# Loading the complex weights of an AFNO layer two modes at a time, in 16 KB runs, with the transform read from two 64-column blocks of x

## The chip, the cores and the metric

The kernel runs on one core of a Trainium2 chip. The metric is the device time of one execution in microseconds (us). The kernel before takes 427.19 us, the median of three runs (427.02 to 427.77). Run to run it moves by about 0.2%.

The engines are PE (TensorE matmul; PEld is its load of the stationary operand), DVE (VectorE), ACT (ScalarE), POOL (GpSimd) and SP (SyncE). The kernel's tiles lie in SBUF, and the results of its matmuls in PSUM, the two memories on the chip; a tile has up to 128 rows, called partitions. The program pins the instructions that matter here (`pin` in the kernel), so that each engine takes them in the order of the program. Nearly all loads are issued by GpSimd and convert f32 to 16 bits on the way; so GpSimd's queue is also the queue of the loads.

## The reference

The layer is linear attention followed by a spectral mix. Batch 8, 8 heads, sequence 576, head size 64, so a model width D of 512. There are 64 Fourier modes, and each has a real and an imaginary weight matrix of 512x512 in f32: together 134 MB, which is most of what is read.

```python
# attention, per batch and head: phi(t) = elu(t) + 1
kv  = einsum('bhsd,bhse->bhde', phi(k), v)
x   = einsum('bhsd,bhde->bhse', phi(q), kv) / (einsum('bhsd,bhd->bhs', phi(q), sum_s phi(k)) + 1e-6)
x   = x.transpose(0, 2, 1, 3).reshape(B, S, 512)
# spectral mix
X   = rfft(x, axis=1)[:, :64]                       # Xr + i Xi
Yr  = einsum('bmd,mde->bme', Xr, w_r) - einsum('bmd,mde->bme', Xi, w_i)
Yi  = einsum('bmd,mde->bme', Xr, w_i) + einsum('bmd,mde->bme', Xi, w_r)
u   = x + irfft(Yr + i Yi, n=576, axis=1)
out = u + relu(u @ w_ch)                            # (8, 576, 512) f32
```

## The kernel before

The program has three parts. Stage A forms x for each of the eight batches and transforms it to the frequency domain (the result is `xt_c`). The stream then multiplies each mode by its weights as they arrive, and fills the gaps with other work. The tail, after the last weight, does the last inverse transforms and the stores.

One load brings one matrix of one mode. Partition p takes rows 4p to 4p+3, that is 4 x 512 f32 = 8 KB in one piece:

```python
W_KEEP, W_PRE = 8, 12      # weight tiles that stay for the stream / for stage A only

def w_load(kk, half, pool, tag, bufs):
    name, src = (("wr", moe_w_r), ("wi", moe_w_i))[half]
    w = pool.tile([128, NDC, D], BF16, ...)                     # NDC = 4
    rows_of = src[kk].rearrange("(p dc) e -> p dc e", dc=NDC)
    ... nc.gpsimd.dma_start(out=w[:, dcs], in_=rows_of[:, dcs, :])
```

In stage A each batch goes through five times `form_x` (four tiles of 128 rows and one of 64) and four times `transform`. `form_x` divides the attention's numerator by its denominator and writes a row of x in its natural order. `transform` uses every fourth column of x as the stationary operand, to fit the rows that a partition of a weight tile holds:

```python
def form_x(b, jj):
    ...                                             # num: PSUM, from 8 matmuls
    nc.vector.reciprocal(out=rden, in_=nv[:, :, :, 64])
    dst = x16s[b][1][orow, :] if tail else x16s[b][0][:, jj, :]
    nc.vector.tensor_tensor(                        # one operation of 128x512
        out=dst.rearrange("p (o c d) -> p o c d", o=2, c=4),
        in0=nv[:, :, :, 0:64], in1=rden....broadcast_to([..., 2, 4, Dh]), op=ALU.mult)

def transform(b, dc):
    for jj in range(NJJ):                           # NJJ = 4
        nc.tensor.matmul(o, x16[:, jj, dc::NDC], fwd_sb[:, jj, :], start=(jj == 0), stop=False)
    nc.tensor.matmul(o, x16t[half, dc::NDC], fwd_sb[half, NJJ, :], start=False, stop=True)
    if dc == NDC - 1:
        nc.vector.tensor_copy(out=xt_v[:, :, 1:3, b, :], in_=xf)
        nc.scalar.mul(out=xt_v[:, :, 0, b, :], in_=xf[:, :, 1, :], mul=-1.0)
```

The order of the loads is the order of the program. `w_next` issues the next early weight load; what is left of the 20 early ones is issued behind stage A's code:

```python
for b in range(B):
    if b + 2 < B:
        load(b + 2)                                 # q, k, v of a later batch
        if b >= 1:
            w_next()
    ...                                             # turn_q, sum_kv, features, exps
    for jj in range(NJJ + 1):
        form_x(b, jj)
        ...                                         # transform(b - 1, ...) in between
for dc in range(NDC):
    transform(B - 1, dc)
while pending:
    w_next()
nc.gpsimd.dma_start(out=wch16, ...)
nc.gpsimd.dma_start(out=pick_sb, ...)               # a constant of the stream's matmuls
```

In the kernel before, GpSimd has nothing in its queue but such issues (and four small constants in the first half microsecond). So it runs ahead of stage A as far as free tiles and the landing of earlier loads allow.

## Time and profile before

| | before |
|---|---|
| time, span of the profiled run | 427.2 us, 425.4 us |
| stage A ends (last transform eviction, that is the copy of its result out of PSUM) | 103 us |
| last weight landed, then the tail | 392.4 us, 33 us |
| weight loads in the steady stretch | one each 2.46 us, 1.05 MB read: 427 GB/s |
| PE busy over the span | 67% |

The page cuts the span into 40 equal slices (10.6 us each here). A digit is the busy share of an engine in tenths; the row DMA is the mean of the 16 DMA engines. GB/s is what they moved, counted after the conversion to 16 bits, so about half of what is read. This is the page of the kernel before:

```profile
PE   1358777887119765666333689778677778998992
DVE  4598999956002755556200433433444244421793
DMA  9999999999999999999999999999999999998797
GB/s 215 208 208 209 209 210 209 212 212 215 218 211 214 214 212 215 214 213 214 212 214 213 213 214 213 214 214 213 213 213 214 214 213 213 213 213 157 250 394 295
```

The DMA is full from the first slice to the 36th. PE and DVE are not: DVE is busy at 80% or more in slices 3 to 8 (stage A), and after stage A both nearly idle in slices 11 and 12. The chain of waits, followed back from the last instruction, says the same by engine:

```profile
DMA 69%; PE 12%; issue 8%; DVE 7%; ACT 2%; POOL 1%; DVEq 0%; POOLq 0%; ACTq 0%
```

So the load stream bounds the kernel, and stage A has slack. How much is to be read from more views. First the groups of instructions (line, engine, operation, tiles, shapes, count; then busy us and mean ns of one; then idle us before them and what ended it):

```profile
L277 DVE TENSOR_TENSOR x<-num,rd 128x512 f16<-128x512 f32 x32 | 22.1, 692 | 1.1
L277 DVE TENSOR_TENSOR x16t<-num,rd 64x512 f16<-64x512 f32 x8 | 5.5, 688 | 0.3
L533 DVE TENSOR_TENSOR x_main<-nw,rdw 128x256 f32<-128x256 f32 x32 | 12.2, 417 | 0.1
L190 ACT ACTIVATE qe<-q 128x1152 f16<-128x1152 f16 (+1 forms) x16 | 17.8, 1157 | 17.8 <-DMA q<-in_q_dram 17.8
```

The first two are the write of x in stage A, 692 ns each, 27.6 us together. The third is an operation of half that width that the stream has, 417 ns. The fourth is ACT's exponential: it waits 17.8 us for q to arrive, so stage A is in part limited by the arrival of its own inputs.

GpSimd's list in order of time (start, duration, operation; in brackets the idle time before it and what ended it), cut:

```profile
64.97 0.56 POOL L108 DMA_DIRECT2D wr<-in_moe_w_r_dram  x1
66.63 0.55 POOL L108 DMA_DIRECT2D wi<-in_moe_w_i_dram  x1 [1.10 <-DMA q<-in_q_dram]
69.48 0.53 POOL L108 DMA_DIRECT2D wr<-in_moe_w_r_dram  x1 [2.30 <-DMA k<-in_k_dram]
...
161.86 0.53 POOL L108 DMA_DIRECT2D wi<-in_moe_w_i_dram  x1 [1.93 <-PE P L359]
```

Four early weight loads are gone by 55 us; the fifth goes out at 65 us and the other fifteen right behind it, most of them before stage A is done. The stream's loads wait for PE to release a tile.

The last eviction of stage A in ACT's list, at 103 us. PE then does the products of the first two modes, to 105.3 us, and one short job, and waits for the constant `pick_sb`, the last of the early loads; it goes on at 125.6 us. I read that as some 22 us of slack for stage A, an estimate. A line of ACT's list, then one of PE's:

```profile
102.94 0.38 ACT L305 ACTIVATE xt_c<-xf 128x256 bf16<-128x256 f32 x1 [2.30 <-DVE xt_c L304]
125.57 0.25 PE L375 MATMUL yt<-pick_sb,ys 128*128 128x16 f16 x4 [15.19 <-DMA pick_sb<-row_pick]
```

### The profile page before, as it was taken

What the parts mean: (1) busy time and instruction counts of PE and PEld (TensorE: products, weight loads), DVE (VectorE), ACT (ScalarE), POOL (GpSimd) and SP (SyncE); (2) the same over time, 40 slices, a digit from 0 to 9 for tenths busy, and PEclk for the clock granted to TensorE, in tenths of its full rate; (3) what the DMA queues carried; (4) which work ended last, traced back from release to release, by engine and by line L of the source; (5) the groups of instructions that cost most, each with busy time, mean ns of one, the idle gap of its engine ahead of it and who ended that gap; (6) DMA issues with size and microseconds to landing.
All of it is one profiled execution on the core that took longest, in us unless ns stands there. A gap on an engine that the chain in (4) does not pass through costs nothing.

```text
span 425.4 us, 6619 instructions
## 1 busy us (share of the span) xinstructions
PE 285.7 (67%) x2692; PEld 160.0 (38%) x2692; DVE 214.5 (50%) x440; ACT 154.1 (36%) x241; POOL 88.3 (21%) x159
## 2 busy tenths in 40 slices
PE   1358777887119765666333689778677778998992
PEld 0246555674003433333111334434334334473420
DVE  4598999956002755556200433433444244421793
ACT  4677776630102100000000244434443354430781
POOL 4222223222201322122112122112122121110000
PEclk9999866565555855555555587989999899999998
DMA  9999999999999999999999999999999999998797
GB/s 215 208 208 209 209 210 209 212 212 215 218 211 214 214 212 215 214 213 214 212 214 213 213 214 213 214 214 213 213 213 214 214 213 213 213 213 157 250 394 295
DMA packets 35502, 93.12 MB, mean 219 GB/s; under 512 B 3024, under 2 KB 15696, under 8 KB 35216
## 3 DMA queue, kind: packets, MB, share of 16 engines
q0 software_dynamic: 31360, 81.48, 98.3%
q1 hardware_dynamic: 4112, 11.22, 7.1%
q8 instruction: 21, 0.34, 0.3%
q14 instruction: 9, 0.07, 0.0%
HBM read 163.93 MB, written 9.44 MB: 407 GB/s over the span
## 4 chain that ended last, share of the span: by engine, by line
DMA 69%; PE 12%; issue 8%; DVE 7%; ACT 2%; POOL 1%; DVEq 0%; POOLq 0%; ACTq 0%
DMA wi<-in_moe_w_i_dram 51%; DMA wr<-in_moe_w_r_dram 9%; DMA k<-in_k_dram 9%; PE acc L641 3%; PE P L359 2%; DVE x L277 2%; PE acc L680 2%; ACT ke L190 1%; PE z L604 1%; DVE ke L203 1%; DVE k L197 1%; PE zb L631 1%; PE zb L630 1%; DVE qe L203 1%; PE yb L626 1%
## 5 line engine op out<-in xcount | busy, mean ns | idle before, releaser
L359 PE MATMUL P<-wi,xt_c 128*32 128x512 bf16 x252 | 37.9, 536 | 38.7 <-DMA wi<-in_moe_w_i_dram 38.6
L370 ACT CAST ys<-P 128x512 f16<-128x512 f32 x31 | 18.2, 586 | 121.6 <-PE P L359 106.8
L108 POOL DMA_DIRECT2D wr<-in_moe_w_r_dram x64 | 34.1, 533 | 130.6 <-PE P L359 91.0
L368 DVE CAST ys<-P 128x512 f16<-128x512 f32 x32 | 22.1, 691 | 72.0 <-PE P L359 49.8
L108 POOL DMA_DIRECT2D wi<-in_moe_w_i_dram x65 | 34.6, 532 | 111.8 <-PE P L359 88.2
L359 PEld LDWEIGHTS <-xt_c 128*32 128x32 bf16 x504 | 28.7, 156 | 75.8 <-issue 64.4
L359 PE MATMUL P<-wr,xt_c 128*32 128x512 bf16 x252 | 37.6, 550 | 24.6 <-DMA wr<-in_moe_w_r_dram 22.5
L563 DVE TENSOR_TENSOR x_main<-ya,x_main 128x512 f32<-128x512 f32 x32 | 22.1, 691 | 43.7 <-PE ya L559 43.6
L582 PE MATMUL eps<-wch,xTw 128*128 128x512 f16 x144 | 41.2, 414 | 0.0
L144 PEld LDWEIGHTS <-qT 64*128 64x128 f16 (+1 forms) x640 | 25.3, 126 | 41.6 <-issue 21.3
L565 ACT CAST x16w<-x_main 128x512 f16<-128x512 f32 x32 | 19.8, 618 | 37.4 <-DVE x_main L563 37.4
L375 PE MATMUL yt<-pick_sb,ys 128*128 128x16 f16 x252 | 16.6, 176 | 24.1 <-DMA pick_sb<-row_pick 15.2
L590 ACT CAST E<-eps 128x512 f16<-128x512 f32 (+1 forms) x40 | 21.3, 543 | 25.5 <-PE eps L582 25.5
L144 PE MATMUL num<-kv,qT 64*128 64x65 f16 (+1 forms) x320 | 13.8, 227 | 20.7 <-ACT kv L250 18.0
L375 PEld LDWEIGHTS <-ys 128*128 128x128 f16 x252 | 12.3, 103 | 39.8 <-issue 16.6
L190 ACT ACTIVATE qe<-q 128x1152 f16<-128x1152 f16 (+1 forms) x16 | 17.8, 1157 | 17.8 <-DMA q<-in_q_dram 17.8
L219 PE MATMUL qTp<-id,qe 128*128 128x128 f16 x144 | 16.7, 309 | 10.1 <-DVE qe L203 9.5
L144 PE MATMUL nw<-kv,qT 64*128 64x65 f16 (+1 forms) x320 | 22.1, 236 | 1.6 <-DVE x_tail L533 1.0
L277 DVE TENSOR_TENSOR x<-num,rd 128x512 f16<-128x512 f32 x32 | 22.1, 692 | 1.1
L190 ACT ACTIVATE ke<-k 128x1152 f16<-128x1152 f16 x16 | 17.7, 1155 | 6.6 <-DMA k<-in_k_dram 6.0
L690 ACT ACTIVATE acc<-acc 128x512 f32<-128x512 f32 x34 | 18.1, 581 | 2.3 <-PE acc L641 1.3
L219 PEld LDWEIGHTS <-qe 128*128 128x128 f16 x144 | 14.5, 146 | 11.2 <-DVE qe L203 9.9
(104 smaller groups left out, 442.5 us busy)
## 6 DMA issues: line engine op xcount, KB each, us to landing
wr<-in_moe_w_r_dram POOLq DMA_DIRECT2D x64, 512.0 KB, 18.6
wi<-in_moe_w_i_dram POOLq DMA_DIRECT2D x63, 512.0 KB, 18.7
k<-in_k_dram POOLq DMA_DIRECT2D x8, 576.0 KB, 14.5
v<-in_v_dram POOLq DMA_DIRECT2D x8, 576.0 KB, 16.6
out_dram<-x_main SPq DMA_DIRECT2D x9, 512.0 KB, 3.1
q<-in_q_dram POOLq DMA_DIRECT2D x7, 576.0 KB, 13.8
out_dram<-x_main SPq DMA_DIRECT2D x2, 1024.0 KB, 5.2
out_dram<-x_main SPq DMA_DIRECT2D x6, 256.0 KB, 3.4
```

Of the source, the lines that this page charges most:

```text
L108: tc.keep_in_program_order(nc.gpsimd.dma_start(out=w[:, dcs], in_=rows_of[:, dcs, :]))
L144: mm = nc.tensor.matmul(num[hpo][orow, c0 : c0 + 65], qT[rows, hpp, h2, cols], kv_sb[rows, hpp, h2, :])
L190: pin(nc.scalar.activation(out=ev[:, c], in_=heads(nm, b, c), func=AF.Exp))
L219: nc.tensor.transpose(qT_ps[:, j].rearrange("p t r -> p (t r)"), phi["q", b][:, hpp, j].rearrange("p o d -> p (o d)"), id16,)
L277: nc.vector.tensor_tensor(out=dst.rearrange("p (o c d) -> p o c d", o=2, c=4), in0=nv[:, :, :, 0:64], in1=rden.unsqueeze(3).broadcast_to([ ...
L359: nc.tensor.matmul(P[dc * 32 : dc * 32 + 32, :], xt_cols(dc, t, kk), w[:, dc, :], start=(t == 1), stop=(t == 0), tile_position=(0, dc * 32),)
L368: fixed(nc.vector.tensor_copy(out=st, in_=P))
L375: nc.tensor.matmul(yt_ps[:, ec, kk % 8, :], st[:, ec * 128 : ec * 128 + 128], pick_sb)
L563: pin(nc.vector.tensor_tensor(out=x, in0=acc, in1=x, op=ALU.add))
L565: pin(nc.scalar.copy(out=x16w[t], in_=x))
L582: nc.tensor.matmul(e_ps, xT[:, c, :], wch16[:, c, :], start=(c == 0), stop=(c == NDC - 1))
L590: pin(nc.scalar.copy(out=dst, in_=e_ps[:, cols]))
```

## The change

The intent is a faster stream: one load now brings the same matrix of two modes, even mode on partitions 0 to 63, odd mode on 64 to 127, so that a partition reads 8 rows, 16 KB in one piece. The rest follows from that. A weight tile's partition now holds 8 rows of D, so the transform has to deliver x by every eighth column; two modes are multiplied at once in the two halves of the array. A stationary operand of two interleaved column sets is refused as one operand when the kernel is built, so x is stored as eight blocks of 64 columns (block k holds the columns k, k+8, k+16, ...), and a ninth block repeats the first, to make all eight windows of two neighbouring blocks contiguous. The diff, cut to its core:

```diff
-    W_KEEP = 8
+    W_KEEP = 4                                     # tiles are twice the size
-        rows_of = src[kk].rearrange("(p dc) e -> p dc e", dc=NDC)
+        rows_of = src[2 * kp : 2 * kp + 2].rearrange("k (p dc) e -> (k p) dc e", dc=NDW)   # NDW = 8
-    W_PRE = 12
+    W_PRE = 6

 def form_x(b, jj):
-            nc.vector.tensor_tensor(
-                out=dst.rearrange("p (o c d) -> p o c d", o=2, c=4),
-                in0=nv[:, :, :, 0:64], in1=..., op=ALU.mult)
+        dst_v = dst[:, 0 : NDW * NP].rearrange("p (k o c d) -> p o c d k", k=NDW, o=2, c=4)
+        for o in range(2):
+                nc.vector.tensor_tensor(
+                    out=dst_v[:, o], in0=nv[:, o, :, 0:64].rearrange("p c (d k) -> p c d k", k=NDW),
+                    in1=..., op=ALU.mult)
+        if jj == NJJ - 1:
+            nc.gpsimd.tensor_copy(out=x16[:, :, NDW * NP :], in_=x16[:, :, 0:NP])
+        if tail:
+            nc.gpsimd.tensor_copy(out=dst[:, NDW * NP :], in_=dst[:, 0:NP])

 def transform(b, ...):
-            nc.tensor.matmul(o, x16[:, jj, dc::NDC], fwd_sb[:, jj, :], ...)     # 20 per batch
+            nc.tensor.matmul(..., x16[:, jj, win * 64 : win * 64 + 128], ...)   # 40 per batch, 8 windows
-            nc.vector.tensor_copy(out=xt_v[:, :, 1:3, b, :], in_=xf)
-            nc.scalar.mul(out=xt_v[:, :, 0, b, :], in_=xf[:, :, 1, :], mul=-1.0)
+            nc.vector.tensor_copy(out=xt_v[HALVES[0], wins, 1:3, b, :], in_=xf[HALVES[0], :, 0])
+            nc.scalar.copy(out=xt_v[HALVES[1], wins, 1:3, b, :], in_=xf[HALVES[1], :, 1])
+        if step == 3:
+                nc.gpsimd.tensor_scalar(out=xt_v[:, :, 0, b, :], in0=xt_v[:, :, 2, b, :],
+                                        scalar1=-1.0, ..., op0=ALU.mult)

 # main loop of stage A
-            if b >= 1:
+            if b % 2 == 1:
                 w_next()
 # product of one mode: 4 tiles of the array -> of two modes: 8 tiles, tile_position=(h * 64, c)
 # ... (last load in four pieces, matmuls that keep PE warm, stores of the tail: adapted)
```

## The prediction

> **What bounds the kernel now.** The DMA stream. In the table of 40 slices the DMA row reads 9 in slices 1 to 36 (208 to 218 GB/s at SBUF, twice that read in f32). The chain of waits is 69% DMA. In the list of GpSimd instructions the weight loads, once steady, go out every 2.46 us per 1.05 MB: 427 GB/s. The last weight lands at about 392.4 us; the tail after it is 33 us. Stage A (attention, transforms) ends at 103 us by the timeline, but GpSimd issues the 15 remaining early weight loads from 66.6 us on, so the stream never stops. PE then idles to 125.6 us: stage A has 22 us of slack.
>
> **What the change does.**
> 1. Runs of 8 KB become 16 KB. The Trainium skill (DMA: Bandwidth & Descriptors, Where 436 GB/s comes from) puts the ceiling at 435 GB/s; the trace is at 427. From q/k/v loads (2.3 KB runs, 2.85 us each at 66 to 83 us) against weights I estimate 4 ns overhead per packet and 15 ns per load: a gain of 0.8%, 2 to 3 us over all weights.
> 2. DVE: two 128x256 operations (0.37 us each) for one 128x512 (0.69 us), two 64-partition evictions for one: about +1 us per batch on a DVE that is 90% busy at 20 to 65 us.
> 3. PE: 40 transform matmuls for 20 per batch, estimate +2 to 3 us per batch, partly in gaps. Mode products keep their array time (eight concurrent tiles for four).
> 4. GpSimd: new copies and a negation per batch, in program order on the queue that also issues every load. The skill (same page, Anatomy of one DMA) says that a DMA's semaphore wait happens on the issuing sequencer, so loads behind a waiting copy are held back. The compiled instruction order shows it: after the loads of batch 7 and the third weight load come the copies and negations of batches 5 to 7, and only then the other seven early weight loads.
>
> **Critical path.** By then 28.3 MB of q/k/v and 6.3 MB of weights are issued, finished by about 84 to 90 us. The next load waits for the last negation, at stage A's end, which grows from 103 to about 115 us (items 2 to 4; loads of batches 3 to 7 also go out some 8 us later). So the DMA idles about 25 us. Sum (estimate): restart at 116.5 us, 61 loads of 4.87 us = 297, w_ch 2.5, tail 33: span 449, time 451 us (+5.5%).
>
> **Prediction.** 451 us, 80% range 440 to 461. Chances: faster by over 2% 0.03, within 2% 0.04, slower by over 2% 0.93.
>
> **What would show it.** (a) Slices: DMA near 0 in about slices 9 to 11, 9 elsewhere. (b) GpSimd list: a gap from about 70 us to 110 or more before the fourth weight load, behind the last negation. (c) Weight loads every 4.85 to 4.91 us in the steady stretch. (d) Last transform eviction at 110 to 120 us. (e) Tail within 2 us of 33. (f) PE not above 90% busy between 250 and 350.
>
> **What would make it wrong.** Stage A slower than thought (GpSimd copies of several us, strided DVE output): +10 us. Stage A no slower: about 439 us. Mode products not running eight at a time: PE limits the last third, +10 us. Stream at the ceiling of 435: 3 us less.

## The result, and the profile after

The changed kernel takes 512.79 us, the median of four runs (511.99 to 513.29), against 427.33 us for the kernel before beside it. The result is correct. The ratio is 1.200 (95% interval 1.198 to 1.202). The prediction was 451 us, with a range of 440 to 461: the direction was right, the size wrong by a factor of 3.6 (85 us of loss for 24).

These are the same lines of the page as before (a slice is now 12.8 us), and the chain by engine:

```profile
PE   1246567576575710285554632578766687998893
DVE  4799999999968200143545530343443443352395
DMA  9939639739000499999999999999999999999598
GB/s 215 207 57 199 103 62 209 114 49 209 4 1 0 91 216 215 213 216 216 215 216 216 215 215 215 216 216 216 215 216 217 215 215 215 216 215 214 121 385 323
```

```profile
DMA 53%; DVE 25%; PE 14%; issue 4%; ACT 2%; POOL 1%; DVEq 0%; ACTq 0%; POOLq 0%
```

The DMA stands idle in slices 11 to 13 and is half idle in several slices before. In the same stretch DVE reads 9 in every slice from 3 to 11: it is saturated from 26 to 140 us, and has a quarter of the chain, where it had 7%. The steady rate of the stream is a little higher (215 to 216 for 213 to 214). What fills DVE shows in its groups:

```profile
L281 DVE TENSOR_TENSOR x<-num,rd 128x256 f16<-128x256 f32 x64 | 78.2, 1410 | 2.0
L281 DVE TENSOR_TENSOR x16t<-num,rd 64x256 f16<-64x256 f32 x16 | 19.5, 1401 | 0.7
L556 DVE TENSOR_TENSOR x_main<-nw,rdw 128x256 f32<-128x256 f32 x32 | 12.5, 418 | 0.2
```

An operation of 128x256 takes 418 ns where it writes contiguously (third line) and 1410 ns where it writes the blocks of x. The write of x took 27.6 us of DVE before and takes 97.7 us now. That is 70 us more, and stage A ended 68 us later. GpSimd's list, cut to the loads and what stands between them:

```profile
114.32 0.56 POOL L113 DMA_DIRECT2D wr<-in_moe_w_r_dram  x1
125.76 0.40 POOL L291 COPY x<-x 128x256 f16<-128x256 f16 x1 [10.88 <-DVE x L281]
128.81 0.23 POOL L293 COPY x16t<-x16t 64x64 f16<-64x64 f16 x1 [2.65 <-DVE x16t L281]
...
171.05 0.85 POOL L319 TENSOR_SCALAR xt_c<-xt_c 128x256 bf16<-128x256 bf16 x1 [4.74 <-ACT xt_c L316]
171.85 0.61 POOL L113 DMA_DIRECT2D wi<-in_moe_w_i_dram  x1
...
291.96 0.53 POOL L113 DMA_DIRECT2D wi<-in_moe_w_i_dram  x1 [4.37 <-PE nw L149]
```

The third weight load goes out at 114.32 us, the fourth at 171.85 us. Between them stand the copies and negations of the last batches, each waiting for DVE or ACT; the fourth load has no wait of its own (no bracket). So two things act together: stage A is much longer, and the early loads are tied to its end. At the other end the tail starts with the last matmuls on weights at 477.15 us; from there to the end of the span it is 33.3 us, as before:

```profile
477.15 0.29 PE L422 MATMUL y_last<-xt_c,wi 64*128 64x16 bf16 x8 [0.34 <-DMA wi<-in_moe_w_i_dram]
```

The span is thus a sum of three parts: restart of the loads, stream, tail. Predicted 116.5 + 299.5 + 33 = 449; measured 171.9 + 305.3 + 33.3 = 510.5. Of the 61 us that were missed, 55 are in the first part.

### The profile page after: what moved, and what is told of

It reads as the page before. It is cut to its first block, busy times and chain, and to the rows that moved or that the text cites. A ratio compares the mean times of both kernels' runs of the same rounds, so it can differ in the third digit from the quotient of the medians.

```text
span 510.5 us, 8063 instructions
## 1 busy us (share of the span) xinstructions
PE 307.2 (60%) x3421; PEld 165.0 (32%) x3421; DVE 279.9 (55%) x487; ACT 156.1 (31%) x250; POOL 68.8 (13%) x121
## 4 chain that ended last, share of the span: by engine, by line
DMA 53%; DVE 25%; PE 14%; issue 4%; ACT 2%; POOL 1%; DVEq 0%; ACTq 0%; POOLq 0%
DMA wr<-in_moe_w_r_dram 35%; DVE x L281 15%; DMA wi<-in_moe_w_i_dram 9%; DMA pick_sb<-row_pick 6%; PE P L379 5%; DMA k<-in_k_dram 3%; DVE x16t L281 3%; PE acc L664 2%; PE acc L703 1%; PE xf L306 1%; DVE ke L207 1%; DVE qe L207 1%; DVE q L201 1%; ACT qT L230 1%; DVE xt_c L315 1%
## 5 line engine op out<-in xcount | busy, mean ns | idle before, releaser
L281 DVE TENSOR_TENSOR x<-num,rd 128x256 f16<-128x256 f32 x64 | 78.2, 1410 | 2.0
L379 PE MATMUL P<-wr,xt_c 64*32 64x512 bf16 x496 | 33.6, 543 | 41.2 <-DMA wr<-in_moe_w_r_dram 36.1
L379 PE MATMUL P<-wi,xt_c 64*32 64x512 bf16 x496 | 30.4, 527 | 37.5 <-DMA wi<-in_moe_w_i_dram 37.4
L379 PEld LDWEIGHTS <-xt_c 64*32 64x32 bf16 x992 | 18.6, 146 | 87.5 <-issue 55.9
L149 PEld LDWEIGHTS <-qT 64*128 64x128 f16 (+1 forms) x640 | 25.6, 129 | 63.6 <-DVE rd L276 27.6
L306 PE MATMUL xf<-fwd_sb,x 128*128 128x128 f16 x256 | 38.5, 305 | 2.2 <-ACT xt_c L316 2.2
L113 POOL DMA_DIRECT2D wr<-in_moe_w_r_dram x32 | 17.1, 534 | 138.4 <-PE P L379 94.1
L113 POOL DMA_DIRECT2D wi<-in_moe_w_i_dram x35 | 18.8, 537 | 111.0 <-PE ya L582 44.8
L613 ACT CAST E<-eps 128x512 f16<-128x512 f32 (+1 forms) x40 | 21.2, 540 | 31.2 <-PE eps L605 31.1
L194 ACT ACTIVATE qe<-q 128x1152 f16<-128x1152 f16 (+1 forms) x16 | 17.8, 1156 | 28.8 <-DMA q<-in_q_dram 28.8
L243 PE MATMUL kvp<-vpad,ke 64*128 64x130 f16 x288 | 17.1, 309 | 13.7 <-DVE x16t L281 10.8
L316 ACT CAST xt_c<-xf 64x256 bf16<-64x256 f32 x16 | 5.9, 367 | 62.0 <-DVE xt_c L315 62.0
L306 PEld LDWEIGHTS <-x 128*128 128x128 f16 x256 | 22.0, 130 | 8.8 <-issue 2.1
```

What stands on the lines that cost most here:

```text
L113: tc.keep_in_program_order(nc.gpsimd.dma_start(out=w[:, dcs], in_=rows_of[:, dcs, :]))
L149: mm = nc.tensor.matmul(num[hpo][orow, c0 : c0 + 65], qT[rows, hpp, h2, cols], kv_sb[rows, hpp, h2, :])
L281: nc.vector.tensor_tensor(out=dst_v[:, o], in0=nv[:, o, :, 0:64].rearrange("p c (d k) -> p c d k", k=NDW), in1=rden[:, o].unsqueeze(2).uns ...
L306: nc.tensor.matmul(xf[:, win % (NDW // 2)].rearrange("p h t m -> p (h t m)"), x16t[half, cols] if jj == NJJ else x16[:, jj, cols], fwd_sb[ ...
L379: nc.tensor.matmul(P[h][c : c + 32, :], xt_cols(dc, t, kp, h), w[HALVES[h], dc, :], start=(t == 1 and dc < NDC), stop=(t == 0 and dc >= ND ...
L613: pin(nc.scalar.copy(out=dst, in_=e_ps[:, cols]))
```

## The experiments

Two theories stand for the first part. The scatter theory: DVE's write of single f16 elements 128 bytes apart is slow, and makes stage A long; the order of GpSimd's queue turns that into idle DMA. The rival: stage A is long because of the added PE and GpSimd work, and DVE waits for those. Beyond that there is the question of how the two causes share the 85 us, and whether the 16 KB runs win anything once both are gone. Runs of rounds 0 are single times, compared with a run of the kernel before on the same chip; their state is given as unknown. The kernel before was between 427.3 and 427.9 us (a single run or the median) on every chip.

Twelve kernels ran. "GpSimd order" in the table means that the copies and negations stand in the queue of the loads.

| run | kernel and edit | time, us | loads resume, us |
|---|---|---|---|
| a_runs16 | after, x written in 16-byte runs | 461.5 | 120.1 |
| a_contig | after, x written contiguously, 64-column stationaries | 472.5 | 130.7 |
| b_order | before, plus idle GpSimd work in the queue | 458.5 | 113.9 |
| b_scatter | before, x written scattered | 471.6 | 167.0 |
| a_both | a_runs16, GpSimd work moved to ACT | 428.2 | short hole at 144.0 |
| a_free | after, GpSimd work moved to ACT | 477.7 | 172.1 |
| b_double | before, transform matmuls twice | 427.1 | no hole |
| a_pick | a_both, `pick_sb` loaded at the start | 427.1 | no hole |
| b_pick | before, `pick_sb` loaded at the start | 430.8 | no hole |
| a_warm | a_pick, more matmuls to keep PE warm | 427.0 | small dent at 140 to 146 (186 GB/s) |
| b_step2 | before, x at steps of 4 and 16 bytes | 434.2 | (operation only) |
| b_step4 | before, x at steps of 8 bytes | 446.7 | (operation only) |

### a_runs16: same layout, other loop order

Only the loop order of the write changes, with d inside, so that eight elements (16 bytes) in a row are written. The layout of x, the matmuls and GpSimd's queue stay. DVE now reads PSUM at a step of 8 elements instead.

```diff
-  dst_v = ... "p (k o c d) -> p o c d k"      in0 ... "p c (d k) -> p c d k"
+  dst_v = ... "p (k o c d) -> p o c k d"      in0 ... "p c (d k) -> p c k d"
```

> Changed kernel, same layout of x, but the two operations that form x walk it with d innermost: 8 neighbours (16 bytes) are written in a row, and PSUM is read with a step of 8. Theory 1 (the cost is the write of single 2-byte elements 128 bytes apart): the operation falls from 1.41 us to 0.37 to 0.6 us, stage A from 171 to about 115 us, time about 445 to 460 us. Rival (it is the four-level pattern, or the permuted order as such, whichever side it is on): the operation stays over 1.2 us and the time near 510 us.

Measured: 461.46 us. The write, and GpSimd's list at stage A's end:

```profile
L281 DVE TENSOR_TENSOR x<-num,rd 128x256 f16<-128x256 f32 x64 | 24.2, 420 | 1.5
```

```profile
119.29 0.85 POOL L319 TENSOR_SCALAR xt_c<-xt_c 128x256 bf16<-128x256 bf16 x1 [2.79 <-ACT xt_c L316]
120.08 0.61 POOL L113 DMA_DIRECT2D wi<-in_moe_w_i_dram  x1
```

The operation falls from 1410 to 420 ns, the loads resume at 120.1 instead of 171.9 us, and the kernel gains 51.3 us. This one line of loop order is the larger part of the loss. The matmuls and GpSimd's copies are all still there, so the rival does not hold for the changed kernel. Nor is it PE's granted clock (the share of full speed that PE was given): from 50 to 165 us it was 0.50 in the changed kernel and 1.00 in a_free below, and stage A ended at 171.0 and 170.2 us. The read of PSUM at a step of 8 elements costs nothing that shows: a_contig below reads it contiguously and its operation takes 420 ns as well. With the write put right the kernel is still 10 us above the predicted 451: the loads resume 3.6 us later than predicted, and the stream takes some 6.7 us longer than the predicted 299.5.

### a_contig: contiguous write, twice the matmuls

The same test from the other side: x is written in its natural order, and the transform takes 64-column stationaries at a step of 8, so two matmuls for one (80 per batch). GpSimd's copies stay, though nothing reads them.

```diff
+  dst_v = dst....rearrange("p (o c d) -> p o c d", o=2, c=4)          # as before, in two halves
-  matmul(..., x16[:, jj, cols], fwd_sb[rows, jj])
+  for h in range(2):                                                  # k = (win + h) % 8
+      matmul(xf[HALVES[h], ...], x16[:, jj, k : k + 63 * 8 + 1 : 8], fwd_sb[rows, jj, h])
```

> Changed kernel, x written in natural order by two plain 128x256 operations, the transform taking 64-column slices with a step of 8; GpSimd's copies are kept in place, though nothing reads them, so that the order of its queue is unchanged. Theory 1 (scattered write costs about 70 us of stage A, the rest of the prediction stands): operation 0.37 us, stage A ends at 108 to 120 us, DMA idle about 25 us, time 442 to 458 us. Rival (the doubled transform matmuls on a half-clock PE stretch stage A): stage A stays above 140 us and the time above 475 us.

Measured: 472.47 us, above the range: a miss. The operation is 420 ns as expected, but stage A ends at 130 us. First the transform's group in the first 175 us of this kernel; then its busy time by engine in a stretch of stage A (stretch, its length, then PE, PEld, DVE, ACT and POOL with counts, PE's granted clock, DMA share, GB/s); then the load behind stage A:

```profile
L306 PE MATMUL xf<-fwd_sb,x 128*64 128x64 f16 x512 | 43.8, 309 | 0.0
```

```profile
90.00:125.00 35.00, 33.70 (x454) 29.21 (x454) 18.68 (x50) 12.24 (x18) 5.22 (x9) 0.50 0.36 68
```

```profile
130.72 0.61 POOL L113 DMA_DIRECT2D wi<-in_moe_w_i_dram  x1
```

PE is busy 33.7 of 35 us: in this experiment PE became stage A's limit. On a PE at full clock, a matmul of 64 columns costs about what one of 128 does: ten of them took 0.87 us (33 to 38 us, clock 1.00) where five of the wider ones took 0.49 us (108 to 111 us of a_both, clock 1.00). At clock 0.50 the ten again took 0.87 us (100 to 110 us), and five wide ones 0.76 (163 to 170 us of the changed kernel). So this run says that the contiguous write is cheap, but it is no clean measure of its worth, and a_runs16 is.

### b_order: the queue order alone, in the kernel before

To the kernel before, GpSimd copies and a negation are added at the places where the changed kernel has them. They write a tile that nobody reads. Nothing else changes.

```diff
+        if jj == NJJ - 1:  nc.gpsimd.tensor_copy(out=idle16, in_=x16[:, :, 0:64])
+        if tail:           nc.gpsimd.tensor_copy(out=idle16[orow, 0, :], in_=dst[:, 0:64])
...
+            nc.gpsimd.tensor_scalar(out=idle16, in0=xt_v[:, :, 0, b, :], scalar1=-1.0, ..., op0=ALU.mult)
```

> Kernel before, with GpSimd copies and a negation into an unused tile at the places of its queue where the changed kernel has them; nothing else. Theory 2 (loads behind a waiting GpSimd instruction are held back): the early weight loads go out only after about 104 us, DMA idles some 20 us between 85 and 106 us, time 443 to 452 us. Rival (queue order harmless): within 3 us of 427 us.

Measured: 458.51 us, 31.2 us more than before and 6.5 above the range. Its page's DMA row, the wait of ACT for q, and GpSimd's list:

```profile
DMA  9999999920999999999999999999999999999597
```

```profile
L191 ACT ACTIVATE qe<-q 128x1152 f16<-128x1152 f16 (+1 forms) x16 | 17.8, 1156 | 28.0 <-DMA q<-in_q_dram 28.0
```

```profile
113.13 0.85 POOL L313 TENSOR_SCALAR idle<-xt_c 128x256 f16<-128x256 bf16 x1 [1.82 <-ACT xt_c L311]
113.93 0.61 POOL L108 DMA_DIRECT2D wi<-in_moe_w_i_dram  x1
```

The hole is where it was expected, but stage A itself ended at 113 instead of 103 us. The loads of q, k and v of later batches stand in the same queue, so they are held as well, and ACT waits 28.0 us for q instead of 17.8, which matches stage A's growth of 10 us. A rival would be that GpSimd's added work slows DVE's operations; but DVE's write of x takes 692 ns in both kernels, and its next costliest operation of stage A 842 ns for 829. The Trainium skill ("DMA: Bandwidth & Descriptors", Anatomy of one DMA) says that a DMA's wait happens on the sequencer that issues it, before the dispatch. The trace of b_scatter (below) agrees: a load's wait of 35.11 us for PE stands in GpSimd's own list. What b_order adds is that any waiting instruction ahead in that queue holds the loads as well: work that nobody uses cost 31 us by where it stood.

### b_scatter: the write alone, in the kernel before

The kernel before with a scattered write: x in four blocks of 128 columns, elements 256 bytes apart in the inner loop, read by the transform as contiguous columns. GpSimd's queue stays as it was.

```diff
+  dst_v = dst.rearrange("p (k o c d) -> p o c d k", k=4, o=2, c=4)     # two operations of 128x256
-  x16[:, jj, dc::NDC]
+  x16[:, jj, dc * 128 : dc * 128 + 128]
```

> Kernel before, with x written scattered (single elements, 256 bytes apart, two 128x256 operations) and the transform reading contiguous columns; GpSimd issues DMA only. Theory 1: the operation takes about 1.4 us, stage A ends at 155 to 170 us, the preloads run on but all buffers are full by about 125 us, so DMA idles some 35 to 45 us: time 460 to 475 us, that is 35 to 50 us less than with both. Rival (stage A slower is hidden by its 22 us of slack and the preloads): time below 440 us.

Measured: 471.59 us, within the range.

```profile
L279 DVE TENSOR_TENSOR x<-num,rd 128x256 f16<-128x256 f32 x64 | 77.8, 1403 | 1.6
```

```profile
131.31 0.54 POOL L422 DMA_DIRECT2D pick_sb<-row_pick  x1 [1.71 <-DMA wi<-in_moe_w_i_dram]
166.96 0.53 POOL L108 DMA_DIRECT2D wr<-in_moe_w_r_dram  x1 [35.11 <-PE P L362]
```

Here the early loads are free to go, and all went by 131 us. Then no tile is left: the next load waits 35 us for PE to use the first weights, which it can only when stage A has ended. A longer stage A thus costs even without the queue, as soon as its slack is spent. (Stage A ended at 165.9 us, 63 us later than before, and the kernel lost 44 us: about 18 us of slack, an estimate.)

### a_free and a_both: GpSimd's work moved to ACT

ACT has room in stage A, and issues no loads. Both kernels move the two copies and the negation there; a_free keeps the scattered write, a_both has the write of a_runs16.

```diff
-  nc.gpsimd.tensor_copy(out=x16[:, :, NDW * NP :], in_=x16[:, :, 0:NP])     # and the tail's
+  nc.scalar.copy(out=x16[:, :, NDW * NP :], in_=x16[:, :, 0:NP])
-  nc.gpsimd.tensor_scalar(out=xt_v[:, :, 0, b, :], in0=xt_v[:, :, 2, b, :], scalar1=-1.0, ...)
+  nc.scalar.mul(out=xt_v[:, :, 0, b, :], in_=xt_v[:, :, 2, b, :], mul=-1.0)
```

> Changed kernel, scattered write kept, GpSimd's copies and negation given to ScalarE. Theory: the two costs overlap. Stage A still ends at 165 to 180 us, but the ten early pairs of loads are in by about 130 us, so the time falls only by what the preloads hold, some 35 to 45 us: 468 to 480 us, level with b_scatter's 472. Rival (with the queue free the rest is hidden): under 450 us.

Measured: 477.70 us, within the range. Stage A ends at 170.2 us, almost as late as in the changed kernel (171.0). The last early load goes out at 116.7 us, and the next load, at 172.1 us, has waited 54.8 us for PE to release a tile:

```profile
172.07 0.53 POOL L113 DMA_DIRECT2D wr<-in_moe_w_r_dram  x1 [54.83 <-PE P L376]
```

> Changed kernel with both suspected causes taken out: d innermost in the write of x, as in a_runs16, and GpSimd's two copies and its negation given to ScalarE, so that GpSimd issues DMA only. If scattered write and queue order are all that cost: stage A ends before about 120 us, DMA reads 9 from slice 1 to 36, time 423 to 427.5 us, level with or up to 1% faster than before (steady weight pairs every 4.89 us for 4.92 give 1.5 us). Rival (doubled transform, pair buffers or the mode products cost as well): over 432 us.

Measured over five rounds: 428.18 us (427.29 to 428.85), against 427.88 for the kernel before; ratio 0.9998 (0.9971 to 1.0024). That is the same, and slightly above the range, a small miss. Four cells can now be set side by side (medians or single times, us):

| | GpSimd in the load queue | GpSimd's work on ACT |
|---|---|---|
| x scattered | 512.8 | 477.7 |
| x in 16-byte runs | 461.5 | 428.2 |

The write costs 51.3 us in the left column and 49.5 in the right; the queue order 35.1 us in the upper row and 33.3 in the lower. The two causes nearly add, and together they are the whole loss: without both, the changed kernel is level with the one before. Put into the kernel before one at a time they cost 44.3 and 31.2 us, in sum 75.5 of the 85.5.

What stops a_both from gaining what its faster stream promised shows in its DMA row and GpSimd's list:

```profile
DMA  8999999999999899999999999999999999997697
```

```profile
143.95 0.53 POOL L113 DMA_DIRECT2D wr<-in_moe_w_r_dram  x1 [13.48 <-PE P L376]
```

There is a small hole in slice 14. Stage A ends at 112 us, and PE must then work off the early weights. Its matmuls need the constant `pick_sb`, which is the last of the early loads and lands at 125.4 us. With tiles of two modes the four kept tiles run out before PE has caught up, and a load waits 13.5 us for it.

### b_double: does the doubled transform cost?

The prediction priced 40 transform matmuls for 20. In the kernel before, each is issued twice.

```diff
+  for again in range(2):
       ...                                          # the same five matmuls
```

> Kernel before, each group of five transform matmuls issued twice (the second starts the sum anew, so the result is right). Theory: doubled transform work lengthens stage A by under 15 us, within its 22 us of slack: stage A ends at 104 to 118 us and the time stays within 3 us of 427. Rival (it stretches stage A past the slack): over 432 us.

Measured: 427.10 us against 427.88. Stage A ends at 109.7 instead of 103 us, and the slack hides it. So the PE half of the rival is worth nothing here.

### a_pick, b_pick and a_warm: is there a version that wins?

a_pick is a_both with `pick_sb` loaded at the start through SyncE's queue; b_pick does that to the kernel before, as the control.

```diff
-  nc.gpsimd.dma_start(out=pick_sb, in_=pick_dr.ap())      # behind the early weights
+  nc.sync.dma_start(out=pick_sb, in_=pick_dr.ap())        # in load(0), behind fwd_sb
```

> a_both, with the 4 KB selection matrix pick_sb loaded from the sync queue at the start instead of behind all early weights on GpSimd's queue. In a_both the stream has a hole of some 3 us near 142 to 146 us, because PE starts the mode products only when pick_sb lands at 125 us and the four pair buffers run out before it has caught up. Theory: the hole closes, DMA is unbroken, time 424 to 426 us, 0.4 to 0.9% faster than before. Rival (the hole has another cause, or the stream is no faster with 16 KB runs): 427 us or more.

Measured over five rounds: 427.06 us (426.30 to 427.45) against 427.86; ratio 0.9977 (0.9963 to 0.9991). A gain of 0.2%, less than expected: a miss. The hole is gone (217 GB/s from 125 to 160 us, 200 in a_both), and the first transpose of the tail starts at 391.9 us, 1.7 us earlier than before. But the tail, counted from that transpose, is longer, 33.4 for 31.8 us. The stretch from 385 to 395 us by engine, first a_pick, then before (columns as above):

```profile
385.00:395.00 10.00, 7.58 (x146) 4.46 (x147) 0.84 (x3) 1.33 (x4) 0.09 (x1) 0.53 0.38 69
```

```profile
385.00:395.00 10.00, 7.83 (x75) 4.17 (x75) 1.83 (x4) 0.81 (x3) 0.00 (x0) 1.00 0.63 122
```

PE's granted clock is 0.53 in a_pick and 1.00 before, just where the tail begins. a_warm tested that with more dummy matmuls before the tail.

```diff
-  FILL = {30: (2, 2, 3), 31: (4,)}
+  FILL = {30: (2, 2, 9), 31: (8,)}
```

> a_pick with more filler matmuls ahead of the last weights (9 for 3 after the last pair but one, 8 for 4 in the last pair). In a_pick the stream ended 1.7 us earlier than before, but PE waited 1.77 us for the last wr with nothing to do and ran at half clock over 386 to 396 us, so the first matmuls of the tail took 0.58 us for 0.40. Theory: with the gap filled the clock stays at 1.0 there, the tail is 31.5 to 32.5 us for 33.4 and the time 425 to 426.3 us, 0.3 to 0.6% faster than before. Rival (the clock falls all the same): 426.5 to 428 us.

Measured over five rounds: 426.96 us against 427.33; ratio 0.9993 (0.9979 to 1.0007), a miss. The clock now stays at 1.0 to 391.7 us, then is 0.59 from there to 395.1 us all the same. The dummy matmuls moved and shortened the dip and did not remove it. (The kept traces show a dip to 0.50 at the start of the tail in every other kernel with loads of two modes, the changed kernel and a_both included; the kernel before has none there.) Its cause stays open. Stage A ended at 114 us here and at 111 in a_pick, with the same code: so much it varies from run to run.

> Kernel before with the same early load of pick_sb, a control. Its stream has no hole, with eight buffers of half the size, so nothing is gained: 426.5 to 428 us. The difference to a_pick is then what 16 KB runs give. Rival: the early selection matrix is what makes a_pick faster, and this one gains as much.

Measured over five rounds: 430.77 us, ratio 1.0069 (1.0054 to 1.0083): slower, a miss. The stream ends as before, but a transfer in the tail waits longer. GpSimd's list, first b_pick, then before:

```profile
398.22 0.56 POOL L801 DMA_DIRECT2D YZ_all<-last  x1 [21.46 <-ACT acc L690]
```

```profile
395.62 0.56 POOL L801 DMA_DIRECT2D YZ_all<-last  x1 [16.54 <-ACT last L797]
```

The same transfer goes out 2.6 us later, behind another instruction of ACT. PE then waits for it, and runs at clock 0.50 from 402 to 404 us, where the kernel before has no such wait and clock 1.00:

```profile
402.06 0.58 PE L641 MATMUL acc<-YZ_all,inv_sb 64*128 64x512 f16 x1 [1.88 <-DMA YZ_all<-last]
```

So the 3 us arise in the tail, after the stream, and are a side effect of the edit; why the wait was placed otherwise was not looked into. They show how far 0.7% may be trusted as the worth of an edit. They also spoil the control: what the 16 KB runs give by themselves, and what the early `pick_sb` gives, cannot be told apart in the 0.2% of a_pick. No version beat the kernel before by 2%.

### b_step2 and b_step4: what law the write follows

All scattered runs so far wrote elements 128 or 256 bytes apart. Here x is written in its natural order at small steps, with free places in between: every 4 and every 16 bytes in b_step2 (the main tiles and the half-height tile), every 8 bytes in b_step4. Fewer early loads pay for the memory, so only the operation is of interest.

```diff
-  sA.tile([128, 2 * NJ * Dh * 2], ...)[:, 0 : NJJ * D]...,  sA.tile([128, D], ...)
+  sA.tile([128, NJJ, D, m], ...)[:, :, :, 0],               sA.tile([128, D, t], ...)[:, :, 0]
-  W_PRE = 12
+  W_PRE = 6          # b_step2: m = 2, t = 8;   b_step4: m = t = 4, W_PRE = 4
```

> The kernel before with the normalised x written one element at a time at small strides (x16 every 4 bytes, the half-height last tile every 16 bytes, one free place after each element), read back at the same strides; fewer early weight loads (6 for 12) pay for the memory, so the total time is not the question, only the duration of the write is. The operation is one of 512 columns again: 692 ns when written contiguously. Theory, every 16-byte line entered costs: between 32 lines (417 ns) and 256 lines (1403 ns) for 256 elements one line more costs 4.4 ns, so x16 (128 lines for 64) takes about 970 ns and the last tile (512 lines) about 2660 ns. Rival A, every element that does not touch its neighbour costs alike: both about 2700 ns. Rival B, only far strides (128 bytes and over) cost: both about 690 ns.

> As the run before with x16 and the last tile both written every 8 bytes (4 early weight loads for 12). Line theory: 256 lines for 64, about 1540 ns for both. Rival A: about 2700 ns. Rival B: about 690 ns.

Measured, first b_step2, then b_step4:

```profile
L275 DVE TENSOR_TENSOR x<-num,rd 128x512 f16<-128x512 f32 x32 | 23.6, 738 | 1.1
L275 DVE TENSOR_TENSOR x16t<-num,rd 64x512 f16<-64x512 f32 x8 | 19.4, 2430 | 0.3
```

```profile
L275 DVE TENSOR_TENSOR x<-num,rd 128x512 f16<-128x512 f32 x32 | 41.9, 1310 | 1.6
L275 DVE TENSOR_TENSOR x16t<-num,rd 64x512 f16<-64x512 f32 x8 | 10.3, 1293 | 0.4
```

Both rivals fall: the cost is neither the same for every lone element nor zero for near ones. But each value also lies some 230 ns below what was expected, and the reason is plain in a table. I take the fixed part of an operation as 142 ns, from 692 ns for 512 contiguous elements and 417 ns for 256; an estimate.

| step of the f16 elements | elements per 16 bytes | measured, less 142 ns, per element | per 16-byte line |
|---|---|---|---|
| 2 bytes (contiguous) | 8 | 1.07 ns | 8.6 ns |
| 4 bytes | 4 | 1.16 ns | 4.7 ns |
| 8 bytes | 2 | 2.28 ns | 4.6 ns |
| 16 bytes | 1 | 4.47 ns | 4.5 ns |
| 128 bytes (after) | 1 | 4.95 ns | 5.0 ns |
| 256 bytes (b_scatter) | 1 | 4.93 ns | 4.9 ns |

The six rows fit, within a tenth, a write that takes the larger of two times, not their sum as I had expected: about 1.07 ns per element, or about 4.6 ns per 16-byte line entered (estimates from this table). With four f16 elements in a line the two are nearly equal (738 ns against 692 for the whole operation). With one the second is four times the first.

## Why the prediction was wrong

**The step that failed is item 2**, "DVE: two 128x256 operations (0.37 us each) for one 128x512 (0.69 us)". The prediction does not say where the 0.37 us come from; DVE's operation of that shape in the trace before is listed at 417 ns, but it writes contiguous rows, and the new one writes single elements 128 bytes apart. It took 1.41 us. Ten such operations per batch are 14 us for an assumed 3.7, on an engine that I had read as 90% busy. Summed over the batches the write grew by 70 us and stage A by 68. a_runs16 shows that it is the write order and not the layout, the matmuls or GpSimd: with 16-byte runs the operation is back at 420 ns and the loads resume at 120 us, close to the 116.5 that was predicted. (The time would still have been 10 us above 451, 461.5 in a_runs16, by the smaller misses below.) "strided DVE output" was named under what would make it wrong, at +10 us, so the risk was seen and not costed; with all of DVE's writes of x at stake it was 51 us. The chance of 0.93 for slower was right, and not by luck: the queue alone, which was foreseen, costs 31 us.

**Item 4, the queue, was right.** Loads behind GpSimd's copies are held to stage A's end, as the compiled order showed beforehand. It is worth 33 to 35 us in the 2x2 table and 31 us in b_order. That it also lengthens stage A, because q, k and v come through the same queue, was named ("some 8 us later", within the 12 us for stage A); in b_order it was 10 us by itself.

**Item 1, the gain of 16 KB runs, was nearly right and small.** One matrix of two modes took 4.89 us against 2 x 2.457 = 4.915, which is 0.5%; over the whole steady stretch the row GB/s rose from 213 or 214 to 215 or 216, about 0.9%. Predicted were 0.8%. The Trainium skill ("DMA: Bandwidth & Descriptors", Where 436 GB/s comes from) puts the ceiling at 435 GB/s; the trace has 427 before and 429 after. There was little left to win.

**Item 3, the transform's matmuls, costs no time**, and was priced too high: doubling them (b_double) made stage A some 7 us longer in all, not 2 to 3 us per batch, and the slack hid that.

The points to look for: (a) the DMA was near 0 in slices 11 to 13 instead of 9 to 11, and not 9 elsewhere: there were holes in slices 3, 5, 6, 8 and 9. (b) The gap in GpSimd's list stood before the fourth weight load behind the last negation, from 114 to 172 us, longer than said. (c) Weight loads every 4.89 us, in the range. (d) The last transform eviction was at 170.6 us and not at 110 to 120: the point that fails, and it names the step. (e) The tail was 33.3 us, as said. (f) PE was busy 25.6 and 27.3 of 50 us between 250 and 350 us, as said; so the products of two modes in the two halves of the array did not make PE the limit.

A second, small miss: the stream took 305.3 us for 299.5. Some 2 us are its first 10 us after the restart, at 173 GB/s; 1.2 us are 4.89 for 4.87 per load; and the last load drains at a falling rate (106 GB/s from 470 to 480 us), about 2.3 us by estimate.

Left open: why PE's clock dips at the start of the tail in the kernels with loads of two modes and not in the kernel before, and with it whether the 1.7 us that the stream gains can be kept.

## What to carry to other kernels

Price an operation by one with the same access pattern, not only the same shape: here a change of layout in SBUF cost nothing or made the operation 3.4 times as long (420 or 1410 ns), by which loop was innermost on the write side. Before giving an engine new work, ask what else stands in its queue; an engine that issues the loads should not wait for the compute stage that those loads are to run ahead of. Where the stream was at 427 GB/s, longer runs won less than one per cent, and every rearrangement that they force has to fit into the slack of the stage that pays for it.

## What the Trainium skill lacked or had wrong

- "SBUF — State Buffer", Specifications (TRN2), says that SBUF lines have 16 bytes, that each cross to a new line pays a penalty, and that two hits per line are needed for full bandwidth. The line size agrees. It gives no size for the penalty. Another page does, for 32-bit streams ("Vector Engine (DVE) Microarchitecture Reference", 5.2 Measured stream behaviour on trn2: 1.71 ns per column where the destination alone hops 4 KiB at every element, 2.50 where it steps 24 words); neither has f16 writes. Here DVE's f16 writes from f32 PSUM took 4.5 to 5.0 ns per line entered, or 1.07 ns per element where that is more. And two hits were not enough: at 8 bytes' step the operation took 1310 ns against 692 ns; only four hits (738 ns) came near full speed.
- The note on lines in "SBUF — State Buffer" (Door 1) says that a non-contiguous PSUM access slows matmuls. It says nothing of DVE's reads, for which no run shows a cost: 420 ns at a step of 8 f32 elements (a_runs16) and 420 ns contiguously (a_contig).
- "DMA: Bandwidth & Descriptors", Where 436 GB/s comes from, says that for transfers between HBM and SBUF the HBM side binds at about 358 GB/s. Here, on one core, the steady weight stream read 427 GB/s before and 429 GB/s after. The sentence lacks the condition that the same page gives under Measured, where a core alone reaches 425 GB/s and the 358 are each core's share when both of a pair stream (no run here has two cores).
- "TensorE: Matmul & The Clock Gate", Part 1, puts the drop of the clock after an idle window of about 3.4 us. In a_pick PE fell to about half clock between 385 and 395 us, although its longest wait there was 1.77 us, and in a_warm with none above 0.45 us. The same page's section on a second failure mode tells of a clock that swings where PE idles briefly and often, but gives no figure for how much. What sets the dip was not found.
